# Loading q, k and v as fp32 over SyncE's hardware queue from the eighth chunk on, in a retention-and-MLP kernel

## The chip, the cores and the metric

The kernel runs on one core of a Trainium2 chip. The metric is the device time of one execution in microseconds; three runs of the kernel before took 313.31, 313.31 and 312.99 us, median 313.31. Beside them there is one profiled execution with its trace: every instruction on the engines TensorE (PE; its weight loads are listed as PEld), VectorE (DVE), ScalarE (ACT), GpSimd (POOL), the instructions of SyncE's queue (SPq), and every DMA packet.

## The reference, cut to what matters

Two layers follow each other. The first is a parallel retention (attention with a decaying causal mask instead of a softmax) over 8 sequences of 576 tokens, 8 heads, 64 features per head; the second is an MLP with an exact GELU over the 4608 tokens.

```python
scores = (1/sqrt(64)) * q @ k.T                     # per batch and head, 576 x 576
gamma  = 1 - 2.0 ** (-5 - arange(8))                # one decay per head
Dmat   = where(i >= j, gamma ** (i - j), 0)
attn   = (scores * Dmat) @ v                        # -> x, 4608 x 512
h      = x @ w_in                                   # 512 x 2048
out    = (0.5 * h * (1 + erf(h / sqrt(2)))) @ w_out # 2048 x 512
```

All inputs and the output are fp32 in memory; the kernel computes its products in bf16.

## The kernel before

**Chunks.** Each sequence is cut into five chunks, four of 128 tokens and one of 64, so there are 40 chunks, numbered 0 to 39; chunks 4, 9, 14 and so on are the short ones. A chunk attends to itself with a masked product of scores, and to all earlier chunks of its sequence through a running 64x64 state per head, `u`. The decay is split: VectorE multiplies v by `dv` before the products (`scaled_v`, line 242, tile `vh`) and the result by `dq` after them (`evacuate`, line 288, tile `x`).

**The steps of a chunk**, by the letters of the planner: load (`load_chunk`, lines 127 to 141); T, turning q and k so that features lie on the partitions (`turn`: chunks 0 to 8 on TensorE, line 213; from chunk 9 on one transposing DMA issued by SyncE, line 207, tile `qkT`); V, scaling v; R, scores on TensorE (line 226) and the mask on VectorE (line 235); S, the products with v and the update of `u` on TensorE (lines 260 and 266); U or the next R, the products with `u` (line 280) and the evacuation. x is turned on TensorE for chunks 0 to 8 and with a transposing DMA on SyncE's queue (line 294) after that, into `xT`, which holds all tokens.

**The MLP** works in 9 blocks of 512 tokens. Its first product (`mlp1_step`, line 314, tile `hT`) needs `xT` and w_in, which is loaded in 8 blocks of 256 columns; ScalarE applies the GELU. Its second (`mlp2_step`, line 343, tile `oT`) needs w_out, loaded in 8 blocks; ScalarE copies the result to `o_sb` (line 349) and SyncE stores it (line 350). The first MLP block is cut into two halves of 256 tokens so that it can begin when chunks 0 and 1 are done.

**The order of the work** is written out by a planner in Python when the program is built: it keeps a clock `now` and picks the next step whose planned time has come. No instruction is reordered afterwards, so each engine and each DMA queue runs in the planner's order and waits where data is late. For loads the planner keeps a second clock, `dma_clock`, to which each full chunk adds 3.0 us and each block of weights 1.38 us.

**Loads before.** Chunk 0 is loaded as fp32 by SyncE (line 84) and cast by VectorE. Every other load is a software DMA issued by GpSimd, which casts to bf16 on the way: q and k of a chunk into one tile `qk_ld`, v into `v_ld`, seven buffers of each (`N_LD = 7`). GpSimd's stream begins with chunks 1 to 3, the 8 blocks of w_in (line 149), chunk 4, four blocks of w_out (line 159), chunk 5, three blocks, chunk 6 and the last block of w_out. From then on the load of chunk i + 7 is issued when step S of chunk i is recorded, and waits until TensorE no longer reads the buffer of chunk i. SyncE's queue carries the three loads of chunk 0, the transposes from chunk 9 on and the stores of the output.

Of the kernel before, what the change touches and what calls it, by code (L numbers as in the profile page):

```python
# [10 lines left out]
FP32 = mybir.dt.float32  # L11
# [6 lines left out]
def kernel(  # L18
# [14 lines left out]
    nc = tc.nc  # L33
    ctx.enter_context(tc.manual_schedule())

    B, H, S, D = q.shape
# [14 lines left out]
    N_PE_TR = 9  # L51
    N_FIRST = 4
    N_LD = 7
    LEAD = 52
    PAIR_FROM = 2
    PAIR_LEAD = 70
# [2 lines left out]

    const_pool = ctx.enter_context(tc.tile_pool(name="const", bufs=1))  # L60
    ld_pool = ctx.enter_context(tc.tile_pool(name="ld", bufs=N_LD))
    tr_pool = ctx.enter_context(tc.tile_pool(name="tr", bufs=9))
    ret_pool = ctx.enter_context(tc.tile_pool(name="ret", bufs=2))
    v_pool = ctx.enter_context(tc.tile_pool(name="v", bufs=5))
# [62 lines left out]
    def load_chunk(i, now=0.0):  # L127
        b, ci, c0, cs = chunks[i]
        qk = ld_pool.tile([128, 2, H, D], BF16, tag="qk", name="qk_ld")
        if i == 0:  # L130
            v_ld = first[2]
            nc.vector.tensor_copy(qk[:, 0], first[0])
            nc.vector.tensor_copy(qk[:, 1], first[1])
        else:
            v_ld = ld_pool.tile([128, H, D], BF16, tag="v", name="v_ld")
            for dst, src in ((qk[:, 0], q), (qk[:, 1], k), (v_ld, v)):
                nc.gpsimd.dma_start(dst[:cs], src[b, :, c0:c0 + cs, :].rearrange("h s d -> s h d"))  # L137
        loaded[i] = (qk, v_ld)
        dma_clock[0] = max(dma_clock[0], now) + 3.0 * cs / C
        v_at = 6.5 if i == 0 else dma_clock[0] + (1.2 if i < N_FIRST else 1.6)  # L140
        land_chunk[i] = (v_at - 1.9, v_at - 0.9, v_at)
# [24 lines left out]
    for i in range(4):  # L166
        load_chunk(i)
    for _ in range(d_ff // W_IN_COLS):
        load_w_in()
    load_chunk(4)  # L170
    for j in range(N_DF // 2):
        load_w_out()
        if j in (3, 6):
            load_chunk(5 + (j == 6))
# [244 lines left out]
    def attention_picks():  # L419
# [8 lines left out]
        if i < nxt["T"] and nxt["S"] == i:  # L428
# [4 lines left out]
            if pick is None or t < PAIR_FROM:  # L433
                if ahead <= LEAD:
                    got.append((r_at, "R", i))
# [38 lines left out]
    while True:  # L474
# [3 lines left out]
        if due:  # L478
            _, kind, i = due[0]
# [6 lines left out]
            elif kind == "S":  # L486
# [3 lines left out]
                now += 0.23 * f + (0.22 if chunks[i][1] + 1 < NCH else 0.0)  # L490
                if i + N_LD < N_CH:
                    load_chunk(i + N_LD, now)
                if chunks[i][1] > 0 or len(mates) > 1:
# [113 lines left out]
```

## Time and profile before

| what | value |
|---|---|
| median of the runs | 313.31 us |
| span of the profiled execution | 444.2 us |
| mean granted TensorE clock in it | 0.658 |
| TensorE busy | 436.6 us, 98% of the span |
| VectorE, ScalarE, GpSimd busy | 101.9, 143.3, 112.4 us |
| software DMA queue | 115792 packets, 17.97 MB |
| hardware DMA queue (SyncE) | 52816 packets, 21.05 MB |

The profiled execution is the longer one because TensorE was granted a clock of about two thirds in it; its span counts from the first to the last instruction. The page gives busy time by engine; the span in 40 slices (11.1 us each), where a digit is the busy share in tenths, with the granted clock and the share of the DMA engines; the DMA queues; the chain of work that ended last; and the costliest groups of instructions. A line of a timeline reads: start in us, duration in us, engine, line, operation, output <- inputs and count, and in brackets the idle time before it with what ended it. A line of DMA issues reads: output <- input, queue, operation and count, KB written by each, and the median us from issue to landing. The two queues' lines give packets, MB, and the time that packets took as a share of the 16 DMA engines; packets overlap on an engine, so this share can pass 100%.

### The profile page before, as it was taken

How to read it: one execution, taken by the hardware profiler on the slowest of the kernel's cores; microseconds unless marked ns; L12 is line 12 of the kernel's file. 1: busy time of each engine (PE TensorE's matmuls, PEld its weight loads, DVE VectorE, ACT ScalarE, POOL GpSimd, SP SyncE). 2: the span in 40 equal slices, each digit the busy share in tenths (PEclk: the TensorE clock that was granted, in tenths of full speed). 3: DMA queues.
4: the chain of work that ended last, by engine and by line, in shares of the span. 5: the costliest groups of instructions: out<-in, count | busy, mean ns of one | idle time of the engine just before them, and what ended most of it. 6: DMA issues, size and time to landing. Idle time of an engine off the chain costs nothing.

```text
span 444.2 us, 6130 instructions
## 1 busy us (share of the span) xinstructions
PE 436.6 (98%) x2522; PEld 204.9 (46%) x2522; DVE 101.9 (23%) x189; ACT 143.3 (32%) x279; POOL 112.4 (25%) x144
## 2 busy tenths in 40 slices
PE   7999999999999999999999999999999999999997
PEld 3676358855534444344433443344434333333334
DVE  4601345345332240034402500063102100000000
ACT  5664025523244213421343124311442134114411
POOL 9878524426242316004620440000000000000000
PEclk8666666666666666666666666666666666666666
DMA  9999979959999989519990991042101200010011
GB/s 136 179 189 178 127 107 144 90 62 158 159 154 72 110 105 155 60 35 167 127 161 1 121 176 47 0 84 72 41 0 49 66 25 0 24 47 26 0 46 49
DMA packets 168636, 39.40 MB, mean 89 GB/s; under 512 B 157600, under 2 KB 164128, under 8 KB 168608
## 3 DMA queue, kind: packets, MB, share of 16 engines
q0 software_dynamic: 115792, 17.97, 59.8%
q1 hardware_dynamic: 52816, 21.05, 22.5%
q8 instruction: 19, 0.31, 0.3%
q14 instruction: 9, 0.07, 0.1%
HBM read 36.70 MB, written 9.44 MB: 104 GB/s over the span
## 4 chain that ended last, share of the span: by engine, by line
PE 95%; DVE 2%; DMA 1%; POOL 1%; issue 1%; ACT 0%; DVEq 0%
PE hT L314 42%; PE oT L343 41%; PE o_ps L260 3%; PE u_ps L266 2%; PE o_ps L280 1%; PE oT L331 1%; DMA qk_ld<-in_k_dram 1%; PE qk_ps L213 1%; PE x_ps L302 0%; DVE x L288 0%; DVE vh L242 0%; DVE qkT L215 0%; POOL qk_ld L137 0%; DVE ret_966 L235 0%; DVE ret_425 L235 0%
## 5 line engine op out<-in xcount | busy, mean ns | idle before, releaser
L137 POOL DMA_DIRECT2D qk_ld<-in_q_dram x39 | 33.5, 859 | 143.7 <-PE u_ps L266 107.4
L349 ACT COPY o_sb<-oT 128x512 f32<-128x512 f32 x35 | 20.5, 585 | 138.4 <-PE oT L343 132.7
L137 POOL DMA_DIRECT2D v_ld<-in_v_dram x39 | 34.0, 872 | 1.4 <-DMA w_in_153<-in_moe_w_in_dram 0.7
L137 POOL DMA_DIRECT2D qk_ld<-in_k_dram x39 | 33.6, 861 | 0.9 <-DMA w_in_151<-in_moe_w_in_dram 0.5
L270 ACT CAST u_sb<-u_ps 128x512 bf16<-128x512 f32 x32 | 18.7, 585 | 43.9 <-PE u_ps L266 43.3
L288 DVE TENSOR_TENSOR x<-o_ps,dq 128x512 bf16<-128x512 f32 (+1 forms) x40 | 26.4, 681 | 24.5 <-PE o_ps L280 14.5
L314 PE MATMUL hT<-xT,w_in_149 128*128 128x512 bf16 (+3 forms) x96 | 25.8, 429 | 0.5 <-DMA w_in_149<-in_moe_w_in_dram 0.5
L314 PE MATMUL hT<-xT,w_in_151 128*128 128x512 bf16 (+3 forms) x96 | 26.2, 431 | 0.0
L314 PE MATMUL hT<-xT,w_in_157 128*128 128x512 bf16 (+3 forms) x96 | 26.2, 432 | 0.0
L314 PE MATMUL hT<-xT,w_in_163 128*128 128x512 bf16 (+3 forms) x96 | 26.0, 432 | 0.0
L314 PE MATMUL hT<-xT,w_in_155 128*128 128x512 bf16 (+3 forms) x96 | 26.0, 428 | 0.0
L314 PE MATMUL hT<-xT,w_in_153 128*128 128x512 bf16 (+3 forms) x96 | 25.5, 423 | 0.3 <-DVE qkT L215 0.3
L314 PE MATMUL hT<-xT,w_in_159 128*128 128x512 bf16 (+3 forms) x96 | 25.5, 427 | 0.0
L314 PE MATMUL hT<-xT,w_in_161 128*128 128x512 bf16 (+3 forms) x96 | 25.5, 428 | 0.0
L242 DVE TENSOR_TENSOR vh<-v_ld,dv 128x512 bf16<-128x512 bf16 x31 | 20.8, 678 | 0.0
L314 PEld LDWEIGHTS <-w_in_159 128*128 128x128 bf16 x96 | 10.7, 117 | 13.4 <-issue 12.2
L314 PEld LDWEIGHTS <-w_in_163 128*128 128x128 bf16 x96 | 10.9, 121 | 12.8 <-issue 12.0
L314 PEld LDWEIGHTS <-w_in_157 128*128 128x128 bf16 x96 | 11.1, 122 | 12.5 <-issue 11.5
L314 PEld LDWEIGHTS <-w_in_149 128*128 128x128 bf16 x96 | 10.8, 119 | 12.9 <-issue 11.2
L314 PEld LDWEIGHTS <-w_in_161 128*128 128x128 bf16 x96 | 10.9, 120 | 12.4 <-issue 10.9
L314 PEld LDWEIGHTS <-w_in_155 128*128 128x128 bf16 x96 | 10.9, 121 | 12.2 <-issue 11.2
L314 PEld LDWEIGHTS <-w_in_151 128*128 128x128 bf16 x96 | 11.0, 120 | 11.5 <-issue 10.6
(814 smaller groups left out, 730.3 us busy)
## 6 DMA issues: line engine op xcount, KB each, us to landing
out_dram<-o_sb SPq DMA_DIRECT2D x35, 256.0 KB, 2.4
qk_ld<-in_q_dram POOLq DMA_DIRECT2D x31, 128.0 KB, 5.0
qk_ld<-in_k_dram POOLq DMA_DIRECT2D x31, 128.0 KB, 5.3
v_ld<-in_v_dram POOLq DMA_DIRECT2D x31, 128.0 KB, 5.5
qk_ld<-in_q_dram POOLq DMA_DIRECT2D x8, 64.0 KB, 5.5
qk_ld<-in_k_dram POOLq DMA_DIRECT2D x8, 64.0 KB, 6.2
v_ld<-in_v_dram POOLq DMA_DIRECT2D x8, 64.0 KB, 5.9
qkT<-qk_ld SPq DMA_TRANSPOSE x31, 5.0
```

The source lines that it names most:

```text
L137: nc.gpsimd.dma_start(dst[:cs], src[b, :, c0:c0 + cs, :].rearrange("h s d -> s h d"))
L213: nc.tensor.transpose(ps[:, hp, :cs], qk[:cs, j, 2 * hp:2 * hp + 2, :], ident[:cs, :cs])
L242: nc.vector.tensor_tensor(vh[:cs], loaded[i][1][:cs], dv[:cs, :, ci:ci + 1].to_broadcast([cs, H, D]), op=ALU.mult)
L260: nc.tensor.matmul(ov[:, e, hp, :], lhsT=s["ret"][e][:, hp, :], rhs=s["vh"][:, 2 * hp + e, :], start=(hp == 0 and mate is None), stop=(ci ...
L266: nc.tensor.matmul(u_ps[0][:, hp, :], lhsT=loaded[i][0][:cs, 1, 2 * hp:2 * hp + 2, :], rhs=s["vh"][:cs, 2 * hp:2 * hp + 2, :], start=(ci = ...
L270: nc.scalar.copy(u, u_ps[0])
L280: nc.tensor.matmul(ov[:cs, e, hp, :], lhsT=s["qkT"][sl, 0, hp, :cs], rhs=s["u"][sl, hp, 64 * e:64 * e + 64], start=False, stop=(hp == HP - 1),
L288: nc.vector.tensor_tensor(x.rearrange("p hp e d -> p e hp d")[:cs], by_parity(i)[:cs], dq.rearrange("p (hp e) c -> p e hp c", e=2)[:cs, :, ...
L314: nc.tensor.matmul(hT[:, :hi - lo], lhsT=w[:, cc, o:o + 128], rhs=xT[:, cc, tok0 + lo:tok0 + hi], start=(cc == 0), stop=(cc == N_DM - 1))
L331: nc.tensor.matmul(oT[:, :hi - lo], lhsT=g_tiles[t, m][:, ts * 128:(ts + 1) * 128], rhs=w_out_sb[m // 2][:, m % 2, lo:hi], start=(m == 0), ...
L343: nc.tensor.matmul(oT, lhsT=g_tiles[t, m][:, ts * 128:(ts + 1) * 128], rhs=w_out_sb[m // 2][:, m % 2, :], start=(m == 0), stop=(m == N_DF ...
L349: nc.scalar.copy(o_sb, oT)
```

## The change

From chunk 7 on (`N_SW = 7`) the three loads of a chunk are issued by SyncE and copy fp32 without a cast. q and k go into a new tile `qk_raw` with four buffers (`N_RAW = 4`, 2 x 512 fp32 per partition each), and GpSimd casts each of them into `qk_ld` with a `tensor_copy`. v goes into an fp32 `v_ld`, and VectorE scales it from there. Chunks 0 to 6 and the weights are loaded as before. The planner's costs are not changed, so TensorE's, VectorE's and ScalarE's orders are the same.

```diff
     N_LD = 7
+    N_RAW = 4
+    N_SW = 7
...
     ld_pool = ctx.enter_context(tc.tile_pool(name="ld", bufs=N_LD))
+    raw_pool = ctx.enter_context(tc.tile_pool(name="raw", bufs=N_RAW))
...
             nc.vector.tensor_copy(qk[:, 1], first[1])
+        elif i >= N_SW:
+            v_ld = ld_pool.tile([128, H, D], FP32, tag="v", name="v_ld")
+            qk_raw = raw_pool.tile([128, 2, H, D], FP32, tag="qk_raw", name="qk_raw")
+            for dst, src in ((qk_raw[:, 0], q), (qk_raw[:, 1], k), (v_ld, v)):
+                nc.sync.dma_start(dst[:cs], src[b, :, c0:c0 + cs, :].rearrange("h s d -> s h d"))
+            for j in range(2):
+                nc.gpsimd.tensor_copy(qk[:cs, j], qk_raw[:cs, j])
         else:
             v_ld = ld_pool.tile([128, H, D], BF16, tag="v", name="v_ld")
             for dst, src in ((qk[:, 0], q), (qk[:, 1], k), (v_ld, v)):
                 nc.gpsimd.dma_start(dst[:cs], src[b, :, c0:c0 + cs, :].rearrange("h s d -> s h d"))
```

## The prediction, made before the changed kernel was run

> **What bounds the kernel now.** I read the page of the profiled execution first, then TensorE's and the queues' timelines over the first 60 us, then the DMA issues with their time to landing, and last the two DMA queues in short windows.
>
> ```profile
> PE 436.6 (98%) x2522; PEld 204.9 (46%) x2522; DVE 101.9 (23%) x189; ACT 143.3 (32%) x279; POOL 112.4 (25%) x144
> PEclk8666666666666666666666666666666666666666
> DMA  9999979959999989519990991042101200010011
> PE 95%; DVE 2%; DMA 1%; POOL 1%; issue 1%; ACT 0%; DVEq 0%
> q0 software_dynamic: 115792, 17.97, 59.8%
> q1 hardware_dynamic: 52816, 21.05, 22.5%
> ```
>
> TensorE is busy 98% of the span and is 95% of the chain that ended last, at a granted clock near 0.65. No removal of work on GpSimd can shorten that chain; the change can only move the moments at which TensorE waits. The DMA row says where: nearly every slice up to about 55 us is full, and later ones are not.
>
> The span, 444.2 us, is 1.42 times the median of the runs, 313.31. Busy TensorE time times clock is 436.6 x 0.658 = 287 us, so the timed runs must be granted a much higher clock. The first 17.5 us follow the transfers and should not shrink; the other 426.7 us shrink to 295.8 if all of them scale, by a factor 0.693, which is a clock of 0.65/0.693 = 0.94. At full clock they would be 277.4, the whole 294.9, and 18.4 us would be waits or time around the span. So I work with factors of 0.65 to 0.69 behind 17.5 us. This matters, as transfers do not get faster with TensorE: slack seen in the profile is smaller in the timed runs.
>
> ```profile
> 0.81 0.44 SPq L84 DMA_DIRECT2D q_90<-in_q_dram  x1
> 1.31 0.58 SPq L84 DMA_DIRECT2D k_92<-in_k_dram  x1
> 1.94 0.96 SPq L84 DMA_DIRECT2D v_94<-in_v_dram  x1
> 59.91 8.24 SPq L350 DMA_DIRECT2D out_dram<-o_sb  x4
> 11.38 0.82 POOL L149 DMA_DIRECT2D w_in_149<-in_moe_w_in_dram  x1
> 16.52 0.87 POOL L149 DMA_DIRECT2D w_in_163<-in_moe_w_in_dram  x1
> 35.17 0.70 POOL L159 DMA_DIRECT2D w_out_194<-in_moe_w_out_dram  x1
> 17.52 1.40 PE L314 MATMUL hT<-xT,w_in_149 128*128 128x256 bf16 x8 [0.54 <-DMA w_in_149<-in_moe_w_in_dram]
> 32.30 1.53 PE L314 MATMUL hT<-xT,w_in_163 128*128 128x256 bf16 x8
> 58.39 0.52 PE L343 MATMUL oT<-w_out_194,g_612 128*128 128x512 bf16 x1
> ```
>
> ```profile
> q_90<-in_q_dram SPq DMA_DIRECT2D x1, 256.0 KB, 3.3
> k_92<-in_k_dram SPq DMA_DIRECT2D x1, 256.0 KB, 4.0
> v_94<-in_v_dram SPq DMA_DIRECT2D x1, 256.0 KB, 4.5
> w_in_149<-in_moe_w_in_dram POOLq DMA_DIRECT2D x1, 256.0 KB, 6.1
> w_in_163<-in_moe_w_in_dram POOLq DMA_DIRECT2D x1, 256.0 KB, 10.2
> w_out_194<-in_moe_w_out_dram POOLq DMA_DIRECT2D x1, 256.0 KB, 8.1
> ```
>
> SyncE's queue is empty between 2.9 and 59.91 us. TensorE waits for w_in_149 at 17.52 us. The last w_in block lands at 16.52 + 10.2 = 26.7 and is used at 32.30: 5.6 us of slack here, but in the timed runs the use comes at 17.5 + 14.8 x 0.65 to 0.69 = 27.1 to 27.8, so 0.4 to 1.1 us. The last w_out block lands at 43.3 and is used at 58.39; in the timed runs at 44.1 to 45.8, so 0.8 to 2.5 us. The weights come nearly as late as they may.
>
> **The change part by part.** *Removed:* the 99 software DMAs of chunks 7 to 39 on GpSimd (its three groups mean 859, 861 and 872 ns), some 85 us of GpSimd. It is 25% busy and waits 107 us for TensorE before these loads: worth 0. What hides it is TensorE's queue of work; I see no place where that cover is gone.
>
> *Added on GpSimd:* 66 casts of 128x512 fp32. No such cast is in the trace. VectorE's cast of the same shape took 0.43 us; GpSimd's 128x512 memset took 0.51 and its 128x128 fp32 select 0.31, four times which is 1.24. So 0.43 to 1.24 us, nearest the memset, which has the shape: 0.6. Two per chunk, 1.2 us, in place of 2.6 us of issuing: 0 on the path, with at most 1.3 us more latency per chunk at the dear end.
>
> *Scaling v from fp32:* 0.69 us for v_94 (fp32) against 0.68 for the bf16 tiles, all on VectorE with 23% busy: 0.
>
> *Moved:* the order of the changed program shows what the diff does not. SyncE's stream runs q32, k32, v32, then chunk 7's q, k, v and chunk 8's q and k with no wait at all. New raw and v buffers are free from the start, where the old loads waited for chunk 0's buffer and stood in GpSimd's stream behind every weight. Chunk 8's v waits only for the scaled v of chunk 1 (VectorE, 11.44 + 0.68 = 12.1 us here), then come 9's q and k; 9's v waits for chunk 2 (15.7), then 10's q and k; 10's v for chunk 3 (19.3). In units of 256 KB (9 is a half chunk) that is 5 + 2 + 2.5 + 1 = 10.5 units put beside the loads of chunks 1 to 3 and all of w_in, in exactly the stretch where the DMA row is full. Loads 11 and 12 follow when GpSimd has cast 7 and 8, behind its issue of w_out_194 at 35.2, beside the last w_out blocks.
>
> What a unit costs the software queue: landings of the three loads on SyncE at 4.1, 5.3 and 6.4 give 1.15 us a unit alone, the dear end. The w_in landings, 17.5 to 26.7 for seven steps of 512 KB read, give 1.32 a step, so 0.66 for 256 KB: the cheap end if bytes alone count. Zero is possible if the engines serve the software queue first. Two windows bear on that, 64 to 65 us (output stores beside loads) and 125.5 to 128 (transposes beside loads), in this order:
>
> ```profile
> q1 hardware_dynamic: 147, 0.27, 78.7%
> q0 software_dynamic: 318, 0.04, 61.8%
> ...
> q0 software_dynamic: 2895, 0.37, 238.9%
> q1 hardware_dynamic: 52, 0.01, 3.3%
> ```
>
> Beside plain stores the software queue moved 318 packets in 1 us, where it moves 2895 in 2.5 us when undisturbed; transposes got next to nothing. The new loads are plain copies like the stores, so I take sharing, at 0.9 us a unit, the middle of 0.66 and 1.15. I let 8 of the 10.5 units be served before the last w_in block: 7.2 us, less 0.7 of slack, 6.5 us on TensorE's path. The rest, 2.5 units and some 2 of loads 11 and 12, reach w_out: (10.5 + 2) x 0.9 = 11.3 less 1.7 slack less the 6.5 already paid is 3.1 at most, 0 at least; I take 1.0, a third, since how many of these units come before the last w_out block is open. TensorE has no idle time behind this in which to win it back: its chain after 20 us is unbroken matmuls.
>
> A rule speaks to the price: "DMA: Bandwidth & Descriptors" in the Trainium skill says, under "Issuing engines are not separate DMA queues", that DMAs of all engines run on the same 16 DMA engines and interleave, which the first window agrees with. Its Specifications give about 358 GB/s from HBM per core, 0.73 us a unit, and 8 units would then be an estimated 5.9 us; the w_in landings show 397 GB/s, so the measurement sets the floor here. Its table "Issuing engine by pattern" has simple loads on SyncE and calls that path generally faster, which would give a gain; the 1.15 us above against 0.87 of a GpSimd issue does not show it.
>
> *Moved past on SyncE:* 18 load DMAs now stand ahead of the first output store (due at 59.91; the latest of their waits, on the scaled v of chunk 5, ends at 49.9 us) and three ahead of chunk 9's transpose, and each later transpose and store has loads before it in the same queue: three of 1.15, 3.5 us per chunk. Chunk 9's transpose was issued at 68.28 and its product is used at 84.60, so this is covered here by 16 us less its landing of 5.0; in the timed runs by 11 less 5.0. Cost 0, to 5 us if the queue backs up.
>
> The sum: 6.5 + 1.0 = 7.5 us on the median, **320.8 us**. In a profile at this clock the 5.6 us of slack takes most of it: 444.2 + 7.2 - 5.6, about 446.
>
> **The rivals.** *A: hidden.* The software queue is served first, as beside the transposes; the 10.5 units trickle in and land by 55 us, when chunk 7 is first needed. Then 0 to 2 us: 313.3 to 315.5. Against it: the stores' window.
>
> *B: faster.* Transposes no longer stand still while software loads run (52 packets in 2.5 us), and from 36 to 52 us, where chunks 7 to 10 were loaded, the engines are lighter. If the timed runs lose part of the 18.4 us there, 1 to 3 us come back: 310.5 to 312.5. It decides only if w_in is delayed by under 1 us. Against it: the profile has no wait for such a transfer on TensorE.
>
> *C: SyncE's queue becomes the bound between 50 and 110 us.* Per chunk it carries loads 3.5, a transpose of qk 1.2 and of x 1.2 (their issue times), and a store 0.4: 6.3 us against a chunk every 3 to 7 us there in the timed runs (TensorE's scores of chunks 8 to 15, at 74.83 to 116.82 us, are 5 to 10 us apart here). It decides once the lateness passes the 6 us above; then 4 to 10 us more, 325 to 331.
>
> **How the numbers follow.** The main case 0.62, A 0.16, B 0.10, C 0.12. A's lower half lies within 0.2% (0.6 us, about what a measurement of this kernel can tell). Faster 0.11, same 0.07, slower 0.82. The main case spans 0.66 to 1.15 a unit: 8 x 0.66 - 1.1 = 4.2 to 12.5 x 1.15 - 0.8 = 13.6, so 317.5 to 327. The range 313 to 329 takes in A and half of C and leaves out B.
>
> **What would show it.** Right: hardware-queue packets between 3 and 25 us; w_in_163's landing (time to landing 10.2) up by 5 us or more; TensorE's first w_in use late by 2 to 5 us; casts under 1.3 us. Wrong: w_in landing as before (A), or waits on TensorE for qkT past 60 us (C). The prediction fails most easily on the share that the hardware queue gets beside w_in.

## The result, and the profile after

The changed kernel takes 336.25 us (median of 4 runs, 335.94 to 336.91) against 313.15 us (312.22 to 313.31) for the kernel before on the same chip: 1.0753 times the time, 95% interval 1.0729 to 1.0776. It is 23.1 us slower, where 7.5 had been forecast. The profiled execution of after took 336.38 us, with a span of 333.9 us and a mean granted clock of 0.99, so its times can be read as those of the timed runs.

The page of after, in the parts shown of before:

```profile
PE 308.9 (93%) x2522; PEld 169.4 (51%) x2522; DVE 105.3 (32%) x189; ACT 142.0 (43%) x279; POOL 72.7 (22%) x111
PEclk9999999999999999999999987999999999999999
DMA  9999999999999999999999999993730220011012
q1 hardware_dynamic: 145024, 44.25, 70.2%
q0 software_dynamic: 23584, 6.36, 18.5%
PE 76%; DMA 16%; POOL 3%; DVE 1%; issue 1%; SPq 0%; ACT 0%; POOLq 0%; ACTq 0%
L143 POOL CAST qk_ld<-qk_raw 128x512 bf16<-128x512 f32 (+1 forms) x66 | 43.3, 664 | 145.6 <-DMA qk_raw<-in_q_dram 98.3
w_in<-in_moe_w_in_dram POOLq DMA_DIRECT2D x8, 256.0 KB, 15.3
```

The packets, 145024 + 23584, are as many as before (115792 + 52816): they only changed queue, and those of the new loads write 256 bytes where the casting ones wrote 128. The DMA row is full up to 225 us (27 slices of 8.35 us).

The profile of before was taken at a clock of 0.658, so before was profiled once more: 312.92 us, span 310.9 us, clock 0.999. All comparisons below are with that trace. Two lines of its page:

```profile
PE 86%; DMA 7%; POOL 2%; DVE 2%; issue 1%; ACT 0%
DMA  9999999999999999999999999917300420021012
```

At the same clock TensorE's share of the chain that ended last fell from 86 to 76%, and that of transfers rose from 7 to 16%. Before has its DMA row full as well, up to 202 us (26 slices of 7.77 us).

> The kernel before, once more, for a profile at whatever clock is granted now. If it is granted about 0.98, the span should be about 311 us (313.15 less the 2.4 us by which the median of the changed kernel, 336.25, exceeds its span, 333.9). All theories expect the last w_in block to land at about 26.7 us and the last w_out block at about 43.3 us, as in the first profile, since transfers do not follow TensorE's clock. The head theory expects little slack: first use of the last w_in block within 1.5 us of its landing.

First the head, in the timelines of after (SyncE, GpSimd, TensorE, in this order):

```profile
2.74 0.92 SPq L141 DMA_DIRECT2D qk_raw<-in_q_dram  x1
8.45 2.66 SPq L141 DMA_DIRECT2D qk_raw<-in_k_dram  x1
15.13 0.37 SPq L141 DMA_DIRECT2D v_ld<-in_v_dram  x1
23.76 0.74 POOL L159 DMA_DIRECT2D w_in<-in_moe_w_in_dram  x1 [1.82 <-DMA v_ld<-in_v_dram]
25.60 1.05 PE L324 MATMUL hT<-xT,w_in 128*128 128x256 bf16 x8 [1.84 <-DMA w_in<-in_moe_w_in_dram]
40.69 1.49 PE L324 MATMUL hT<-xT,w_in 128*128 128x256 bf16 x12 [0.70 <-DMA w_in<-in_moe_w_in_dram]
```

and TensorE's and GpSimd's in the second profile of before:

```profile
17.54 1.05 PE L314 MATMUL hT<-xT,w_in 128*128 128x256 bf16 x8 [0.93 <-DMA w_in<-in_moe_w_in_dram]
29.70 2.36 PE L314 MATMUL hT<-xT,w_in 128*128 128x256 bf16 x20
11.38 6.00 POOL L149 DMA_DIRECT2D w_in<-in_moe_w_in_dram  x8
```

SyncE issues five loads from 2.74 us on without a wait. GpSimd issued all of w_in by 17.4 us before; now its last block is issued at 23.76 and lands at 40.64, 13.6 us later than the 27.00 of before, which TensorE first used at 27.96: 1.0 us of slack, as expected. TensorE waits for w_in eight times, and from 34 us on it runs each block as it lands.

The second place is late. The groups of waits on TensorE, after:

```profile
PE sc L236 <- DMA qkT<-qk_ld: 7.6, 5, 3.8
PE hT L324 <- DMA w_in<-in_moe_w_in_dram: 5.8, 8, 1.8
PE qk_ps L223 <- DMA qk_ld<-in_q_dram: 3.0, 3, 1.2
```

The columns are total, times and longest, in us. Before:

```profile
PE hT L314 <- DMA w_in<-in_moe_w_in_dram: 0.9, 1, 0.9
PE sc L226 <- DMA qkT<-qk_ld: 0.9, 2, 0.6
```

The start of the scores of a chunk on TensorE's timeline shows when the time was lost:

| scores of chunk | before, us | after, us | late by |
|---|---|---|---|
| 9 | 65.6 | 78.3 | 12.7 |
| 20 | 118.1 | 134.1 | 16.0 |
| 28 | 173.4 | 189.5 | 16.1 |
| 32 | 204.7 | 227.4 | 22.7 |

So there are two losses: some 13 us in the head, and some 10 us at transposes that land late, 3.3 us of it up to 134 us and 6.6 us around 200 us.

### The profile page after: what moved, and what is told of

It reads as the page before. It is cut to its first block, busy times and chain, and to the rows that moved or that the text cites. A ratio compares the mean times of both kernels' runs of the same rounds, so it can differ in the third digit from the quotient of the medians.

```text
span 333.9 us, 6161 instructions
## 1 busy us (share of the span) xinstructions
PE 308.9 (93%) x2522; PEld 169.4 (51%) x2522; DVE 105.3 (32%) x189; ACT 142.0 (43%) x279; POOL 72.7 (22%) x111
## 3 DMA queue, kind: packets, MB, share of 16 engines
q1 hardware_dynamic: 145024, 44.25, 70.2%
q0 software_dynamic: 23584, 6.36, 18.5%
## 4 chain that ended last, share of the span: by engine, by line
PE 76%; DMA 16%; POOL 3%; DVE 1%; issue 1%; SPq 0%; ACT 0%; POOLq 0%; ACTq 0%
PE hT L324 33%; PE oT L353 33%; DMA w_in<-in_moe_w_in_dram 5%; DMA v_ld<-in_v_dram 4%; DMA qkT<-qk_ld 3%; PE sc L236 3%; PE o_ps L270 2%; DMA qk_raw<-in_q_dram 2%; DMA qk_raw<-in_k_dram 2%; PE u_ps L276 2%; POOL qk_ld L147 2%; PE o_ps L290 1%; PE oT L341 1%; DMA xT<-x 1%; POOL qk_ld L143 1%
## 5 line engine op out<-in xcount | busy, mean ns | idle before, releaser
L324 PE MATMUL hT<-xT,w_in 128*128 128x512 bf16 (+4 forms) x768 | 132.0, 326 | 6.7 <-DMA w_in<-in_moe_w_in_dram 5.8
L353 PE MATMUL oT<-w_out,g 128*128 128x512 bf16 x560 | 131.5, 384 | 0.0
L328 ACT ACTIVATE g<-hT 128x512 bf16<-128x512 f32 (+4 forms) x192 | 93.4, 491 | 50.9 <-PE hT L324 49.0
L324 PEld LDWEIGHTS <-w_in 128*128 128x128 bf16 x768 | 69.2, 98 | 63.8 <-DMA w_in<-in_moe_w_in_dram 7.7
L353 PEld LDWEIGHTS <-g 128*128 128x128 bf16 x560 | 52.6, 99 | 58.2 <-issue 2.7
L143 POOL CAST qk_ld<-qk_raw 128x512 bf16<-128x512 f32 (+1 forms) x66 | 43.3, 664 | 145.6 <-DMA qk_raw<-in_q_dram 98.3
L245 DVE TENSOR_TENSOR ret<-sc,msk 128x512 bf16<-128x512 f32 x64 | 41.1, 682 | 86.5 <-PE sc L236 86.5
L298 DVE TENSOR_TENSOR x<-o_ps,dq 128x512 bf16<-128x512 f32 (+1 forms) x40 | 26.3, 681 | 23.1 <-PE o_ps L290 15.9
L252 DVE TENSOR_TENSOR vh<-v_ld,dv 128x512 bf16<-128x512 f32 (+1 forms) x31 | 23.2, 753 | 18.2 <-DMA v_ld<-in_v_dram 18.2
L236 PE MATMUL sc<-qkT 64*128 64x128 bf16 (+1 forms) x320 | 15.2, 225 | 7.8 <-DMA qkT<-qk_ld 7.6
L270 PE MATMUL o_ps<-vh,ret 128*128 128x64 bf16 x256 | 13.4, 198 | 0.0
L227 ACT COPY qkT<-qk_ps 128x512 bf16<-128x512 bf16 x8 | 4.7, 586 | 10.5 <-PE qk_ps L223 10.5
```

Source lines behind the costliest of these rows:

```text
L143: nc.gpsimd.tensor_copy(qk[:cs, j], qk_raw[:cs, j])
L236: nc.tensor.matmul(sc[e][:cs, hp, :cs], lhsT=qkT[sl, 1, hp, :cs], rhs=qkT[sl, 0, hp, :cs], start=True, stop=True)
L245: nc.vector.tensor_tensor(r[:cs, :, :cs], sc[e][:cs, :, :cs], msk[:cs, :, :cs].to_broadcast([cs, HP, cs]), op=ALU.mult)
L252: nc.vector.tensor_tensor(vh[:cs], loaded[i][1][:cs], dv[:cs, :, ci:ci + 1].to_broadcast([cs, H, D]), op=ALU.mult)
L270: nc.tensor.matmul(ov[:, e, hp, :], lhsT=s["ret"][e][:, hp, :], rhs=s["vh"][:, 2 * hp + e, :], start=(hp == 0 and mate is None), stop=(ci ...
L298: nc.vector.tensor_tensor(x.rearrange("p hp e d -> p e hp d")[:cs], by_parity(i)[:cs], dq.rearrange("p (hp e) c -> p e hp c", e=2)[:cs, :, ...
```

## The experiments

The theory after the result: two causes, both the DMA engines' time for packets of 256 bytes. In the head the early loads take engine time from w_in (theory H); later SyncE's one queue carries loads, transposes and stores, and the transposes land late (theory Q). Rivals: GpSimd's casts and SyncE's waits in order. Each run is compared with before on its own chip.

**The head loads held back.** One column of the last w_out block is copied into chunk 7's raw tile, so SyncE's loads wait until the weights have landed. Nothing else changes.

```diff
             qk_raw = raw_pool.tile([128, 2, H, D], FP32, tag="qk_raw", name="qk_raw")
+            if i == N_SW:
+                nc.gpsimd.tensor_copy(qk_raw[:, 0, 0, 0:1], w_out_sb[-1][:, 0, 0:1])
```

> The changed kernel, with one addition: a copy of one column from the last w_out block into chunk 7's raw tile on GpSimd, so that SyncE's loads start only when all weights have landed. Head theory (the early loads delay the weights by 14 us: the last w_in block lands at 40.6 us instead of 26.7): landings of w_in and w_out return to 26.7 and 43.3 us, and 12 to 14 us of the 23.1 us come back, so 322 to 324 us; what is left is the queue behind 66 us. Rival (the single hardware queue alone is the cause, and the lost time at the head would be made good later): back by under 4 us, 332 to 336 us. Rival (no second cause): all of it back, 313 to 315 us.

338.04 us, ratio 1.0722 (1.0643 to 1.0801): no better than after. The last w_in block landed at 27.63 us, so the head was cured, but TensorE's waits moved (waits view of this run):

```profile
PE sc L238 <- DMA qkT<-qk_ld: 20.8, 8, 7.7
```

The expectation (322 to 324 us) was missed because it treated the two losses as independent. The longest wait, 7.7 us, is that of chunk 9, whose scores start at 74.3 us instead of 65.6. Its second cast and its transpose, in GpSimd's and SyncE's timelines of this run:

```profile
55.21 0.61 POOL L145 CAST qk_ld<-qk_raw 64x512 bf16<-64x512 f32 x1 [0.53 <-DMA qk_raw<-in_k_dram]
70.24 1.56 SPq L219 DMA_TRANSPOSE qkT<-qk_ld  x1
```

Between the two, SyncE's queue issues the loads of chunks 11 to 13 and four stores: the loads, which begin at 43.8 us here, crowd it ahead of the transpose. The run from chunk 13 on, below, leaves chunks 7 to 12 to software and has chunk 9 only 1.4 us late. So the 24.3 us by which this run is slower than before include what the hold itself crowds together, and are no price of the queue alone.

**Only the head.** Chunks 7 to 10 over SyncE, all later ones by software as before.

```diff
-        elif i >= N_SW:
+        elif N_SW <= i < N_SW + N_RAW:
```

> Only chunks 7 to 10 are loaded as fp32 by SyncE; from chunk 11 on GpSimd's software DMA as before. Head theory: the last w_in block lands near 40 us as in the changed kernel, and 12 to 15 us are lost against before: 325 to 328 us. Queue theory (the loss arises because every later load, transpose and store shares SyncE's queue): 313 to 318 us. If the two causes simply add, this run's loss and that of the gated run make 23 us together.

325.42 us, ratio 1.0362 (1.032 to 1.0404): 11.7 us more than before, 10.0 to 12.7 by the interval. The last w_in block lands at 40.84 us, and TensorE has no wait for qkT left. The head's loss as such is this large.

**A smaller dose in the head.** Chunks 7 and 8 alone, 6 units of 256 KB.

```diff
-        elif i >= N_SW:
+        elif N_SW <= i < N_SW + 2:
```

> Chunks 7 and 8 alone are loaded over SyncE's queue: 6 units of 256 KB beside the head instead of 10.5 (the run with chunks 7 to 10 lost 11.7 us, its last w_in block landed at 40.8 us). Head theory, a price per unit: 6/10.5 of it, 6 to 8 us, so 319 to 321 us, and a w_in landing of 34 to 35.5 us. Rival (the mere presence of a second queue slows the software queue, whatever its size): 323 to 326 us. Rival (only the units that coincide with w_in count, not those beside chunks 1 to 3): 313 to 315 us.

320.12 us, ratio 1.0235 (1.02 to 1.027). The last w_in block lands at 34.03, 7.0 us late: 1.17 us a unit, against 13.84 / 10.5 = 1.32 in the run before this one. The loss follows the number of units, as theory H had it (319 to 321 us). A price for the mere presence of a second queue (323 to 326 us) and one for the units beside w_in alone (313 to 315 us) both fall.

**Only the later chunks.** Nothing beside the weights; hardware loads from chunk 13 on.

```diff
-    N_SW = 7
+    N_SW = 13
```

> The hardware loads begin with chunk 13, which stands behind four stores in SyncE's queue, so that nothing is put beside the weights or beside chunks 7 to 12. Queue theory (from 66 us on SyncE's queue gets 3.45 us of loads per chunk beside 2.5 us of transposes and stores, and cannot keep up): waits for qkT on TensorE of 8 to 15 us, 321 to 328 us. Rival (the late waits of the changed kernel are an echo of the late head): 313 to 315 us.

330.19 us, ratio 1.059 (1.0554 to 1.0625), more than the 321 to 328 expected. w_in lands at 27.73 us, and the waits are those for qkT (waits view; the profiled execution is the fastest, 326.63 us):

```profile
PE sc L236 <- DMA qkT<-qk_ld: 11.3, 9, 3.0
```

The queue alone costs 17.9 us. The two parts, 11.7 and 17.9, come to 29.6 and not 23.1. What relieves the queue of after is not shown: the loads of four chunks are in early there, and TensorE asks for all that follows some 12 us later. No run separates the two.

**The loads on ScalarE's queue.** From chunk 11 on.

```diff
-    N_SW = 7
+    N_SW = 11
...
-                nc.sync.dma_start(dst[:cs], src[b, :, c0:c0 + cs, :].rearrange("h s d -> s h d"))
+                nc.scalar.dma_start(dst[:cs], src[b, :, c0:c0 + cs, :].rearrange("h s d -> s h d"))
```

> Loads as before up to chunk 10; from chunk 11 on fp32 loads over the hardware queue of ScalarE instead of SyncE's, with GpSimd's casts. ScalarE issues them in its own order behind chunk 4, so nothing is put beside w_in. If SyncE's in-order queue (transposes and stores standing behind loads) is the second cause, TensorE's waits for qkT and xT (about 10 us between 92 and 200 us) vanish: 313 to 316 us, a microsecond or two for 0.6 us of issuing per load on ScalarE. If the 16 DMA engines' time is the cause (fp32 loads of 256-byte packets cost more than the casting ones), the waits stay: 320 to 324 us. If the casts on GpSimd are, they stay too.

362.23 us, ratio 1.1541 (1.1486 to 1.1596). It missed, by a wait that neither theory had (waits view):

```profile
PE sc L236 <- ACT o_sb L359: 10.8, 4, 4.1
PE hT L324 <- ACT g L328: 10.0, 5, 3.2
PE sc L236 <- ACT g L328: 8.8, 3, 4.9
```

In ScalarE's order GELUs and copies stand behind the loads, and loads wait. In ScalarE's timeline of this run, for one, a load is issued at 118.87 us, 4.7 us after the one before it, and the GELU behind it starts after 7.16 us of idle time:

```profile
118.87 0.37 ACTq L141 DMA_DIRECT2D v_ld<-in_v_dram  x1
119.29 2.06 ACT L328 ACTIVATE g<-hT 128x512 bf16<-128x512 f32 x4 [7.16 <-DMA qkT<-qk_ld]
```

The run does not tell whether another hardware queue would have helped.

**The fp32 loads on GpSimd's software queue.** From chunk 13 on, with the casts one chunk later.

```diff
-    N_SW = 7
+    N_SW = 13
...
-                nc.sync.dma_start(dst[:cs], src[b, :, c0:c0 + cs, :].rearrange("h s d -> s h d"))
-            for j in range(2):
-                nc.gpsimd.tensor_copy(qk[:cs, j], qk_raw[:cs, j])
+                nc.gpsimd.dma_start(dst[:cs], src[b, :, c0:c0 + cs, :].rearrange("h s d -> s h d"))
+            to_cast.append((qk, qk_raw, cs))
+            while to_cast and (len(to_cast) > 1 or i == N_CH - 1):
+                d, r, n = to_cast.pop(0)
+                for j in range(2):
+                    nc.gpsimd.tensor_copy(d[:n, j], r[:n, j])
```

> As the run from chunk 13 on, but the fp32 loads are issued by GpSimd on its software queue, and each chunk's casts are put behind the next chunk's loads. Same bytes, packets and casts; the transposes and stores have SyncE's queue to themselves again. If the shared in-order queue is the cause, it falls to 313 to 317 us. If fp32 packets cost the DMA engines more than casting ones whatever the queue, or if the casts are the cause, it stays with the run from chunk 13 on, within 3 us.

354.18 us in its fastest run, up to 394.97; the clock granted to TensorE was 0.91 to 0.96, so only its waits are read. In the profiled run TensorE waited 58.1 us for qkT, and a transpose took 14.7 us to land in the median. It missed both expectations and separates nothing: without the cast a software packet is another kind (46672 packets for 27.40 MB), and GpSimd's casts wait in order with its issuing.

**Larger packets.** After, with every load as 128 packets of 2 KB instead of 1024 of 256 bytes.

```diff
-                nc.sync.dma_start(dst[:cs], src[b, :, c0:c0 + cs, :].rearrange("h s d -> s h d"))
+                nc.sync.dma_start(dst[:cs].rearrange("p h d -> p (h d)"),
+                                  src[b].rearrange("h s d -> (h s d)")[c0 * H * D:(c0 + cs) * H * D].rearrange("(p f) -> p f", f=H * D))
```

> The changed kernel with each fp32 load reading the same number of bytes from one contiguous stretch: 128 packets of 2 KB in place of 1024 of 256 bytes. The values land in the wrong places, so the output is not the reference's; the instructions, waits, casts and bytes are the same. Packet theory (what the loads cost the 16 DMA engines is the time of their 256-byte packets, 18 ns each, some 1.15 us per 256 KB, where 2 KB packets take 97 ns, 0.78 us): both losses shrink, to 318 to 328 us, with the last w_in block landing by 36 us instead of 40.6. Rival (casts on GpSimd, and SyncE's waits in order, are what holds the transposes): the late waits for qkT stay, 332 to 336 us. Rival (bytes alone count): no change.

322.53 us, ratio 1.031 (1.0273 to 1.0347): 14 us less than after, with the same bytes, instructions, waits and casts. No wait of 0.5 us or more for qkT is left. The last w_in block lands at 33.93 us, 6.9 late, 0.66 us a unit. What remains is the head, with one wait of 2.5 us for w_out.

**Larger packets without the head.** The same, from chunk 13 on.

```diff
-    N_SW = 7
+    N_SW = 13
...
-                nc.sync.dma_start(dst[:cs], src[b, :, c0:c0 + cs, :].rearrange("h s d -> s h d"))
+                nc.sync.dma_start(dst[:cs].rearrange("p h d -> p (h d)"),
+                                  src[b].rearrange("h s d -> (h s d)")[c0 * H * D:(c0 + cs) * H * D].rearrange("(p f) -> p f", f=H * D))
```

> Chunks 13 to 39 over SyncE as in the run from chunk 13, but each load as 128 packets of 2 KB (same bytes, instructions, casts and waits; the values land in wrong places). Theory P (the time that 256-byte packets take is the whole cost, and beside the head there is nothing): hardware packets of after took 70.2% of 333.9 us, with 2 KB packets 56.9% of 321.0 us, 51.8 us less for 88.5 units of 256 KB, so 0.58 a unit less than 1.15; the queue then carries 3 x 0.57 + 1.15 + 0.6 + 0.7 = 4.2 us per full chunk against one every 5.3 us, and no wait for qkT is left: 312 to 314.5 us. Theory O (the place in SyncE's order or GpSimd's casts cost time by themselves): waits for qkT of 3 us or more stay, 317 to 330 us.

312.23 us, ratio 0.9985 (0.9959 to 1.0012): as fast as before. From chunk 13 on all of the change is there, 54 casts, loads ahead of transposes, v scaled from fp32, and it costs nothing. One wait of 0.9 us for qkT is left, as much as before has in all. So the second loss is that of the 256-byte packets, and not of the casts or of the order in SyncE's queue. One thing changes with the packets: a 2 KB packet reads memory in one stretch where eight short ones read it in eight places. No run holds the size and changes the places. The queues between 66 and 126 us show what limits them (packets, MB, time of the packets as a share of 16 engines). Before:

```profile
q0 software_dynamic: 33695, 4.24, 142.3%
q1 hardware_dynamic: 16318, 5.36, 61.8%
```

After:

```profile
q1 hardware_dynamic: 42453, 11.74, 112.2%
```

From chunk 13, 256-byte packets:

```profile
q1 hardware_dynamic: 42593, 11.54, 112.6%
```

From chunk 13, 2 KB packets:

```profile
q1 hardware_dynamic: 23219, 14.57, 112.5%
```

Before, both queues moved 50013 packets in these 60 us. With everything in the hardware queue, after and the run from chunk 13 move the same 42500, and 41238 and 41316 in the next 60 us: this is taken as the queue's limit, some 0.7 packets per ns (the run with the head loads held back moved 41766 and 40194). The packets that before moved in 60 us take 50013 / 42500 x 60 = 71 us, 11 late; the scores of chunk 20 start at 129 us in the run from chunk 13, against 118. With 2 KB packets more bytes come through.

**Part of the loads.** From chunk 13 on, q and k alone over SyncE (first diff), and v alone (second); the rest by software.

```diff
-            v_ld = ld_pool.tile([128, H, D], FP32, tag="v", name="v_ld")
+            v_ld = ld_pool.tile([128, H, D], BF16, tag="v", name="v_ld")
...
-            for dst, src in ((qk_raw[:, 0], q), (qk_raw[:, 1], k), (v_ld, v)):
-                nc.sync.dma_start(dst[:cs], src[b, :, c0:c0 + cs, :].rearrange("h s d -> s h d"))
+            for e, dst, src in ((nc.sync, qk_raw[:, 0], q), (nc.sync, qk_raw[:, 1], k), (nc.gpsimd, v_ld, v)):
+                e.dma_start(dst[:cs], src[b, :, c0:c0 + cs, :].rearrange("h s d -> s h d"))
```

```diff
-            qk_raw = raw_pool.tile([128, 2, H, D], FP32, tag="qk_raw", name="qk_raw")
-            for dst, src in ((qk_raw[:, 0], q), (qk_raw[:, 1], k), (v_ld, v)):
-                nc.sync.dma_start(dst[:cs], src[b, :, c0:c0 + cs, :].rearrange("h s d -> s h d"))
-            for j in range(2):
-                nc.gpsimd.tensor_copy(qk[:cs, j], qk_raw[:cs, j])
+            for e, dst, src in ((nc.gpsimd, qk[:, 0], q), (nc.gpsimd, qk[:, 1], k), (nc.sync, v_ld, v)):
+                e.dma_start(dst[:cs], src[b, :, c0:c0 + cs, :].rearrange("h s d -> s h d"))
```

> From chunk 13 on q and k as fp32 over SyncE with the casts on GpSimd, v as a software load that casts to bf16. Theory Q1 (what SyncE's queue alone carries, 2 x 1.15 + 1.15 + 0.6 + 0.7 = 4.75 us per full chunk against a chunk every 5.3 us): no backlog, 313 to 316 us. Theory Q2 (all the packets share the 16 engines: 4.75 + 0.83 = 5.6 us against 5.3): 0.3 us per chunk over 27 chunks less some lead, 317 to 322 us, waits for qkT of 3 to 9 us. If each load has its price whatever stands beside it: two thirds of the 17.9 us of all three loads, 325 us.

> From chunk 13 on v alone as fp32 over SyncE; q and k stay software loads that cast to bf16, and GpSimd casts nothing. Theories Q1 (queue 3.6 us per full chunk) and Q2 (all packets 3.6 + 1.66 = 5.3 us against 5.3): 312.5 to 315 us, waits for qkT under 3 us. If each load has its price whatever stands beside it: a third of 17.9 us, 319 us.

q and k alone: 317.95 us, ratio 1.015 (1.0092 to 1.0208), waits for qkT 5.2 us, as the account of both queues had it. v alone: 319.75 us, ratio 1.021 (1.0168 to 1.0253), where both accounts had expected 312.5 to 315. A fixed price per load had 319 for v alone, but 325 for q and k. In the chain of work that ended last, in the run with v alone (start, duration), stand two transposes:

```profile
75.13 9.82 DMA qkT<-qk_ld
102.64 7.57 DMA qkT<-qk_ld
```

The hardware queue moved only 25530 packets in the 60 us here, far from its limit, yet transposes took 10 and 8 us to land beside 22338 software packets. No account holds for both runs: the limit of the queue accounts for the full change, and the price of a mixture stays open.

## Why the prediction was wrong, point by point

**Right: the place and the order.** SyncE's loads issue from 2.74 us on with no wait, 8v only after the scaled v of chunk 1, in the order foretold, and w_in is late for it. The time to landing of the last w_in block rose by 6.7 us, from 10.2 to 16.88, past the 5 us named; TensorE's first use of w_in was 8 us late, more than the 2 to 5 named. The timed runs have a clock near 1.0; 0.94 to 1 had been worked out from the profile at 0.658.

**Wrong in size: "8 of the 10.5 units", "0.9 us a unit".** By the landing of the last w_in block at 40.64 us, the hardware queue of after had moved 13934 packets, and 3120 of them are chunk 0's. The other 10814 are all 10.5 units. The delay was 13.6 us, so a unit cost 1.30. The term was 7.2 and measured 13.6. Less 1.0 us of slack that is 12.6, and chunk 9 of after is 12.7 us late; the run with the head alone ends 11.7 us late. The queues of after between 26.6 and 40.64 us show how the two were served:

```profile
q0 software_dynamic: 3897, 1.51, 86.0%
q1 hardware_dynamic: 3903, 0.98, 53.0%
```

As many packets of one queue came through as of the other, so the early loads did not give way to w_in, as rival A had supposed. Earlier, between 8 and 19 us, it was 6395 of the software queue to 4030, where the software queue alone moved 8647 in before. The bounds, 0.66 and 1.15, were both read from true rows, but the step took their middle. The dear one was the row of the same form: chunk 0's loads, of 256-byte packets. The prediction calls them alone, but from 4 to 6.5 us of that profile the software queue moved 880 packets beside 1285 of theirs; alone, from 2.5 to 4 us, they moved 1548 in 1.5 us, 1.0 us a unit. So 1.15 was already a price beside software loads, and near the 1.17 to 1.32 measured. The cheap one was that of w_in, whose source rows are 1 KB (256 columns of fp32); 0.66 is just what the loads cost once their packets were 2 KB. The middle was a price for neither.

The Trainium skill, "DMA: Bandwidth & Descriptors", section "Specifications", asks for transfers of at least 512 bytes to reach line rate. The run with 2 KB packets in the head agrees, 0.66 against 1.30 us for the same 256 KB. The same page's section "Issuing engine by pattern" sends simple loads to SyncE and calls that path generally faster. It does not hold here: these loads over SyncE made 313.15 us into 336.25, and with 2 KB packets from chunk 13 on they gained nothing (312.23).

**Wrong: "Moved past on SyncE: cost 0".** This failed as rival C said, and its signs came, waits on TensorE for qkT past 60 us. Its price, 4 to 10 us, was nearly right: after is some 11 us above the run with the head alone. What failed is the term of 0, which came to 11.4 us in after (23.1 less 11.7), and with it the chance of 0.12 for C. The term rested on two steps. The DMA row was read as full up to 55 us and not later; but of its 19 slices from 55 to 266 us 13 are at 9, and at full clock the row is full up to 202 us. And the working had 6.3 us of queue time per full chunk against a chunk every 3 to 7 us, and called this covered by 11 us less 5. But a queue that carries more than it can move loses a little with every chunk; a cover of fixed length only delays that. Chunks 9 to 33 of before follow each other by 5.8 us on average (65.6 to 205.0 us), so there was nothing to spare, and the demand should have been added up over the 33 chunks.

**Right: nothing for casts, v, the removed DMAs.** A cast took 0.66 us on average (0.6 foretold), scaling v from fp32 0.73 us (0.69 foretold); the run with 2 KB packets from chunk 13 has them all at the time of before. Freeing GpSimd gained nothing, so rival B fell, and A fell with the w_in waits. The 1.0 us for w_out did not show: TensorE has no wait for w_out in after, being late itself by then; with 2 KB packets it has one, of 2.5 us.

## What to carry to other kernels

Price a transfer from a row with the same packet size, not from one with the same bytes, and count everything that can be issued without a wait as served at once, packet for packet, beside what is urgent. For a queue that carries loads and transposes in one order, set the sum of its packets over the whole stretch against what it moves at its limit; slack per chunk does not answer that. Two losses found apart need not add: here 11.7 and 17.9 us alone made 23.1 together. And a run that holds transfers back to cure one stage can crowd the next.

## What the runs showed of the hardware that was not expected

**A late transfer costs its wait and then a slower clock.** The windows of after around the wait of 3.83 us that ends at 199.8 us (window, length, busy time of PE, PEld, DVE, ACT and POOL, granted clock, DMA share, GB/s):

```profile
190.00:195.00 5.00, 5.00 (x55) 2.67 (x53) 3.71 (x7) 0.96 (x2) 0.28 (x1) 1.00 0.90 211
195.00:200.00 5.00, 1.17 (x24) 0.80 (x24) 1.29 (x2) 0.21 (x1) 2.11 (x4) 0.84 1.05 184
200.00:205.00 5.00, 5.00 (x34) 2.24 (x31) 3.68 (x6) 0.42 (x1) 0.00 (x0) 0.50 0.77 169
205.00:210.00 5.00, 5.00 (x44) 2.72 (x42) 0.69 (x1) 1.92 (x4) 1.23 (x2) 0.97 1.26 228
```

For 5 us after the wait TensorE is fully busy at a clock of 0.50, which is 2.5 us of work lost on top of the 3.8: 6.3 us of the 6.6 by which the lateness grew between chunks 28 and 32. The Trainium skill, "TensorE: Matmul & The Clock Gate", section "Why this matters for your kernels", warns of gaps above about 3 us for this reason, and this row agrees. With the head loads held back the clock was 0.50 from 71 to 76 us, around the end of its wait of 7.7 us. In the run with the head alone the eight matmuls behind a wait of 2.9 us took 1.89 us instead of 1.05. The eight matmuls behind the wait of 1.84 us for w_in in after took 1.05 us, so no drop there. No single length divides the two: behind a wait of 2.45 us for w_out, in the first run with 2 KB packets, the windows have 0.81 and then 0.56, while behind one of 3.04 us at 193.6 us in the run from chunk 13 the clock stays at 1.00. So from about 2.5 us on the length of a wait can be too small a price for it.

**A clock of 1.00 in the windows need not be the clock.** In after the profile has 1.00 for all windows up to 24 us. But four matmuls that turn q or k take 0.61 to 0.63 us there, up to 21.1 us, where they take 0.40 us from 7.5 us on in before. They take 0.61 us as well in the run with the head alone, whose windows have 0.50 from 8 to 18 us. So the durations show a slower TensorE that the granted clock of this profile does not.

**One queue for everything moves fewer packets than two.** The same count of packets came through at 50013 in 60 us over a software and a hardware queue, and at 42500 over the hardware queue alone, though the first were smaller when written. The two mixtures lie between: 46674 with q and k on SyncE, 47868 with v alone.
